# Cluster attention and two MLPs on one core: one transfer for the centroids, and the second pair's preparation moved forward in the opening

## Chip, cores and metric

The kernel runs on one core of a Trainium2 chip. The time is that of the device for one execution, in microseconds (us), and less is better. Engines are called TensorE, VectorE, ScalarE, POOL (GpSimd) and SyncE; in rows they are PE (PEld for its weight loads), DVE, ACT, POOL and SP.

## What is computed

Per batch and head, each query and key is assigned to the nearest of 16 centroids by cosine similarity, and a query attends only to keys of its own cluster. The result goes through two MLPs (softplus, then a hard swish), all in float32.

```python
batch, n_heads, seq, head_dim, n_clusters = 2, 8, 768, 64, 16
q_assign = np.argmax(np.einsum('bhsd,hcd->bhsc', q_n, c_n), axis=-1)   # q_n, k_n, c_n: of length 1
k_assign = np.argmax(np.einsum('bhsd,hcd->bhsc', k_n, c_n), axis=-1)
mask = q_assign[:, :, :, None] == k_assign[:, :, None, :]
scores = np.where(mask, scale * np.matmul(q, k.transpose(0, 1, 3, 2)), -1000000000.0)
attn = softmax(scores)
x = np.matmul(attn, v)                       # then (1536 tokens, 512)
x = softplus(x @ w_in1) @ w_out1             # 512 -> 2048 -> 512
h = x @ w_in2
out = (h * np.clip(h + 3.0, 0.0, 6.0) / 6.0) @ w_out2
```

## The kernel before

**Pairs and steps.** Two heads make a pair, with the 64 dimensions of each on one half of the 128 partitions; there are eight pairs (two batches of four). Float32 values are kept as a high and a low part and a product is the sum of three matmuls (high by high, low by high, high by low). The attention runs in steps: one step `s` is one head's tile of 128 queries, so a pair has 12 steps. In step `s`, in this order: `expo(s+1)` on ScalarE (exponentials of 128 by 768 scores), `row_max(s+2)` on VectorE (tile `nm`), `flip(s, 0)` and `flip(s, 1)` (three transposes each on TensorE into tile `t`, the high part on ScalarE as `pth`, the low part on VectorE as `ptl`), `scores(s+3)` on TensorE (four matmuls), and `weigh` on TensorE (probabilities by v) from step 3 on. The scores have two banks, so scores(s) waits for expo(s-2).

**Order.** The whole attention is in a manual schedule: each engine executes its instructions in the order in which the program writes them. Work beside the steps is put in by `at(s, where, fn)`: it is written at place `where` (0 to 6) of step `s`; place 3 is between the two flips, place 4 behind them and ahead of the scores. The loop begins at step -3, and the first scores(0) are written ahead of it. All transfers but the centroids' are issued by SyncE, in order; SyncE stops at a transfer whose data or target isn't ready, and all later ones stand behind it.

**Preparing a pair.** `load_qk` brings q and k (384 KB each), into one buffer each, so that the next pair's must wait until the low part of this pair's is computed. `p_split_hi` and `p_split_lo` make the parts, a half of 384 columns at a time: high parts of pairs 0 and 1 on ScalarE; low parts of pair 0 and of pair 1's q on VectorE, of pair 1's k on POOL. `p_centroids` writes the pair's centroids into the weights `cwh` and `cwl` (four short POOL steps). `p_sims` is three matmuls of 384 columns; parts 0 and 2 take q's two halves, 1 and 3 k's. `p_sims_out` evacuates them on ScalarE, scaled by the centroids' inverse norms `c_r`, `p_back` transposes them, and five steps on VectorE and POOL (`p_max`, `p_equal`, `p_rank`, `p_best`, `p_first`) give one-hot rows, which `p_onehot` transposes and `p_mask` evacuates. `assemble` copies the parts into the operands Q[i] and K[i] of head i (five transfers between SBUF places, 1.15 MB), and `assemble_mask` adds the one-hot rows (four small ones). Q[0] and K[0] may be overwritten once scores(5) have read them, and scores(12), the first of the second pair, need them again. `p_values` splits v on POOL (four steps for a pair).

**The opening.** The first pair is done differently: its centroids come in five transfers issued by ScalarE (`cT`, transposed, and four copies of the rows `c_sb`), their norms are computed by `c_root` (a logarithm and an exponential on ScalarE, then two rounds of four short VectorE steps) and `c_unit`; Q[0] and K[0] are put together by `assemble_first`, one head is ranked by `one_head(0)` and the other by `one_head(1)` in step 0, and `place` writes the one-hot rows from PSUM straight into Q[0] and K[0]. `warm` are transposes of the identity whose result isn't used. `bank(0, ...)` takes PSUM banks in turn from the list `spare`. The banks of the tag "t" are those that the flips use later.

**Beside it.** Weights of the first MLP are fetched in pieces (`fetch_w`, two transfers of 512 KB) and converted by `convert_abs` (ScalarE), three `convert_bits` (VectorE), `convert_parts` (ScalarE) and `convert_rest` (POOL).

Of the kernel before, what the change touches and what calls it, by code (L numbers as in the profile page):

```python
# [22 lines left out]
def cluster_attention_then_two_mlps(  # L23
# [3 lines left out]
    k: bass.AP,  # L27
    v: bass.AP,
    centroids: bass.AP,
    centroid_rows: bass.AP,  # L30
    w_in1: bass.AP,
    w_out1: bass.AP,
    w_in2: bass.AP,
# [3 lines left out]
    nc = tc.nc  # L37
# [2 lines left out]
    B, NPAIR, _, S = q.shape  # L40
    D = v.shape[-1]
    H = 2 * NPAIR
    C = centroids.shape[-1]
    NJ = S // P
    NT, DM = out.shape
    DFF = w_in1.shape[1]
# [8 lines left out]
    def f32(ap):  # L55
        return ap.bitcast(F32)
# [105 lines left out]
    def attention():  # L162
        with ExitStack() as st, ExitStack() as st_ld, ExitStack() as st_ps:
# [18 lines left out]
            SL = 2 * NJ  # L182
            raws = {}

            def load_qk(n, nm):
                b, p = order[n]
                src = {"q": q, "k": k}[nm]
                t = ld.tile([P, S], F32, tag=nm, name=nm)
                if n == 0:
                    for hf in range(2):  # L190
                        nc.sync.dma_start(t[:, hf * HALF:(hf + 1) * HALF], src[b, p, :, hf * HALF:(hf + 1) * HALF])
                else:
                    nc.sync.dma_start(t, src[b, p])
                raws[n, nm] = t
# [5 lines left out]
                raws[n, "v"] = t  # L200


            cT = cb.tile([P, NPAIR, C], F32, name="cT")
            nc.scalar.dma_start(cT, centroids)
            c_sb = sm.tile([P, HALF], F32, tag="sT", name="c_sb", bufs=1)[:, :NPAIR * D].rearrange("p (n d) -> p n d", d=D)
            for r in range(0, P, 2 * C):
                nc.scalar.dma_start(c_sb[r:r + 2 * C], centroid_rows)
            load_qk(0, "q")
            load_qk(0, "k")

            Q = [qk.tile([P, 2, S], F32R, name=f"Q{i}") for i in range(2)]
# [33 lines left out]
                    pl, tag = ps_p, "prep"  # L245
                return pl.tile(shape, dt, tag=tag, name=name)

            spare = [(ps_t, "t"), (ps_t, "t"), (ps_v, "pv"), (ps_p, "prep")]

            def p_split_hi(n, nm, hf):  # L250
                d = prep.setdefault(n, {})
                if hf == 0:
                    d[nm] = tuple(tp.tile([P, S], F32R, tag=f"{u}{nm}", name=f"{u}{nm}") for u in ("hi", "lo"))
                dst = slice(hf * HALF, (hf + 1) * HALF)
                hi, raw = d[nm][0][:, dst], raws[n, nm][:, dst]
                if n < 2:
                    nc.scalar.activation(hi, raw, AF.Copy, scale=scale if nm == "q" else 1.0)
                else:
                    if nm == "q":
                        nc.gpsimd.tensor_scalar(raw, raw, scale, None, ALU.mult)  # L260
                    nc.gpsimd.tensor_copy(hi, raw)

            def p_split_lo(n, nm, hf):
                d = prep[n]
                dst = slice(hf * HALF, (hf + 1) * HALF)
                hi, lo, raw = d[nm][0][:, dst], d[nm][1][:, dst], raws[n, nm][:, dst]
                if nm == "q" and n < 2:
                    nc.vector.scalar_tensor_tensor(lo, raw, scale, f32(hi), ALU.mult, ALU.subtract)
                else:
                    e = nc.gpsimd if n else nc.vector  # L270
                    e.tensor_tensor(lo, raw, f32(hi), ALU.subtract)
# [239 lines left out]
            def at(s, where, fn, *a):  # L511
                extra.setdefault((s, where), []).append((fn, a))
# [5 lines left out]
            for n in range(NP):  # L518
# [32 lines left out]
                    at(o + 5, 5, p_values, n, 0)  # L551
                    at(o + 6, 4, p_values, n, 1)
                elif n:
                    at(-2, 2, p_split_lo, n, "q", 0)
                    at(-1, 2, p_split_lo, n, "q", 1)
                    at(-1, 1, p_centroids, n)
                    at(-1, 1, p_split_hi, n, "k", 0)
                    at(-1, 1, p_split_lo, n, "k", 0)
                    at(0, 1, p_split_hi, n, "k", 1)
                    at(0, 1, p_split_lo, n, "k", 1)  # L560
                    at(1, 3, p_sims, n, 0)
                    at(1, 3, p_sims, n, 2)
                    at(1, 5, p_sims, n, 1)
                    at(1, 5, p_sims, n, 3)
                    at(2, 1, p_sims_out, n)
                    at(2, 3, p_back, n)
                    at(2, 6, p_max, n)
                    at(3, 2, p_equal, n)
                    at(3, 4, p_rank, n)
                    at(4, 2, p_best, n)  # L570
                    at(5, 2, p_first, n)
                    at(6, 3, p_onehot, n)
                    at(6, 6, p_mask, n)
                    at(5, 3, assemble, n, 0)
                    at(7, 1, assemble_mask, n, 0)
                    at(10, 5, assemble, n, 1)
                    at(11, 4, assemble_mask, n, 1)
                    at(1, 1, load_v, n)
                    at(7, 0, p_values, n, 0)
                    at(10, 3, p_values, n, 1)  # L580
# [56 lines left out]
            for f in range(1, NFA):  # L637
                at(2 * f, 6, fetch_w, 0, f)
            piece = pieces0[0]
            at(2, 0, convert_abs, *piece)  # L640
            at(2, 1, convert_bits, *piece, 0)
            at(2, 3, convert_bits, *piece, 1)
            at(2, 5, convert_bits, *piece, 2)
            at(4, 1, convert_parts, *piece, False)
            at(4, 6, convert_rest, *piece)
            piece = pieces0[1]
            at(7, 0, convert_abs, *piece)
            at(7, 0, convert_bits, *piece, 0)
            at(9, 0, convert_bits, *piece, 1)
            at(11, 4, convert_bits, *piece, 2)  # L650
            at(12, 4, convert_parts, *piece, False)
# [50 lines left out]
                nc.vector.tensor_scalar(c_n, c_n, 1e-6, None, ALU.add)  # L702
                nc.vector.reciprocal(c_r, c_n)

            def assemble_first():

                d = prep[0]
                (qh, ql), (kh, kl) = d["q"], d["k"]
                lo_rows, hi_rows = slice(0, D), slice(D, P)
                nc.gpsimd.tensor_copy(Q[0][lo_rows], qh[lo_rows].unsqueeze(1).to_broadcast([D, 2, S]))  # L710
                nc.sync.dma_start(f32(Q[0])[hi_rows, 0], f32(ql)[lo_rows])
                nc.sync.dma_start(f32(K[0])[hi_rows, 0], f32(kh)[lo_rows])
                nc.scalar.activation(K[0][lo_rows, 0], kh[lo_rows], AF.Copy)
                nc.gpsimd.tensor_copy(K[0][lo_rows, 1], kl[lo_rows])

            p_centroids(0)
            clear(1)
            p_split_hi(0, "q", 0)
            p_split_lo(0, "q", 0)
            p_split_hi(0, "q", 1)  # L720
            p_split_lo(0, "q", 1)
            for step in range(3):
                c_root(step)
            c_unit()
            for hf in range(2):
                p_split_hi(0, "k", hf)
                p_split_lo(0, "k", hf)
            assemble_first()
            load_qk(1, "q")
            load_qk(1, "k")  # L730
            for c in (0, 2, 1, 3):
                p_sims(0, c)
            p_sims_out(0)
            p_back(0)
            load_v(0)
            for _ in range(8):
                nc.tensor.transpose(warm[:, :P], ident, ident)

            oh = sm.tile(full, BF16, tag="oh", name="oh", bufs=1)
            nc.vector.memset(oh, 0.0)  # L740
# [14 lines left out]
                nc.vector.tensor_tensor(ov, eq, mx2.unsqueeze(2).to_broadcast(half), ALU.is_equal)  # L755

            one_head(0)
            po = [None, None]
            for e in range(2):
                p_onehot(0)  # L760
# [17 lines left out]
            place(0, 1, 1)  # L778
            scores(0)
            place(1, 0, 1)  # L780
            assemble(0, 1)
            p_split_hi(1, "q", 0)
            p_split_hi(1, "q", 1)
            p_values(0, 0)
            fetch_w(0, 0)
            p_values(0, 1)
# [197 lines left out]
```

## Time and profile before

| what | value |
|---|---|
| time, median of 3 runs | 794.99 us (794.67 to 795.22) |
| the profiled execution: its time, and its span | 795.4 us, 793.6 us |
| granted TensorE clock, mean | 0.991 of full speed |
| TensorE busy | 772.8 us, 97% |
| VectorE, ScalarE, POOL busy | 462.1, 413.8, 155.0 us |
| moved by DMA | 69.75 MB |

The profile is of one execution. Its span runs from the first to the last instruction; the time of that execution holds the span and 1.8 us around it. Positions are counted from the start of the span. A clock of 1.00 is TensorE's full 2.4 GHz, 0.50 is 1.2 GHz. In the timeline a line may merge several instructions (x3), and what stands in brackets is how long the engine had been idle and what ended that.

### The profile page before, as it was taken

To read this page: it belongs to the slowest core of one execution; us is meant where nothing else is said; L and a number is where in the kernel's file an instruction comes from. 1 tells how busy PE (TensorE), PEld (TensorE's weight loads), DVE (VectorE), ACT (ScalarE), POOL (GpSimd) and SP (SyncE) were. 2 spreads that over 40 slices of the span, in tenths; PEclk is the share of its full clock that TensorE was granted. 3 is DMA by queue.
4 is the path that set the end of the run, shared out by engine and by line. 5 is a ranking of instruction groups with operands and counts; after the bars stand their busy time and mean duration, and the time that the engine had idled before them with its cause. 6 is when DMAs were issued, how large, how long until landed. Compare 5 with 4: busy or idle time off the path is not lost.

```text
span 793.6 us, 10533 instructions
## 1 busy us (share of the span) xinstructions
PE 772.8 (97%) x3829; PEld 645.7 (81%) x3829; DVE 462.1 (58%) x793; ACT 413.8 (52%) x827; POOL 155.0 (20%) x225
## 2 busy tenths in 40 slices
PE   6799999999999999999999999999999999999998
PEld 5688888888888778888888888888888888888886
DVE  4888888888898899921111257779852322232222
ACT  3689889889899766532121344555432222222221
POOL 3467568568423300000000000000000000000000
PEclk8899999999999999999999999999999999999999
DMA  6675484484375390000000265650000100010001
GB/s 156 192 202 136 127 193 110 128 198 109 83 173 190 127 370 1 1 0 1 1 0 1 82 208 178 196 185 1 1 1 0 54 1 0 1 54 0 1 1 53
DMA packets 37876, 69.75 MB, mean 88 GB/s; under 512 B 4384, under 2 KB 22464, under 8 KB 37824
## 3 DMA queue, kind: packets, MB, share of 16 engines
q1 hardware_dynamic: 37488, 68.91, 30.2%
q8 instruction: 30, 0.49, 0.2%
q10 hardware_dynamic: 336, 0.16, 0.1%
q14 instruction: 22, 0.18, 0.1%
HBM read 46.30 MB, written 3.19 MB: 62 GB/s over the span
## 4 chain that ended last, share of the span: by engine, by line
PE 85%; ACT 5%; DVE 4%; DMA 3%; issue 1%; POOL 1%; SPq 0%; ACTq 0%; DVEq 0%; POOLq 0%
PE h L158 32%; PE y L865 17%; PE y L863 16%; PE s L397 6%; PE t L427 6%; PE pv L442 6%; PE psm L297 2%; ACT pr L413 2%; DMA Q<-hiq 1%; ACT pth L431 1%; DMA K<-hik 1%; ACT mk L356 1%; DVE val L108 1%; ACT xs L455 0%; ACT xs L457 0%
## 5 line engine op out<-in xcount | busy, mean ns | idle before, releaser
L158 PE MATMUL h<-xhi,pi 128*128 128x512 f32 x768 | 238.8, 392 | 2.2 <-DVE pi L133 2.2
L158 PEld LDWEIGHTS h<-xhi,pi 128*128 128x128 f32 x768 | 143.7, 188 | 34.3 <-DVE pi L133 3.0
L844 DVE TENSOR_TENSOR glo<-g,ghi 128x512 fp32r<-128x512 f32 x96 | 66.3, 691 | 146.3 <-ACT ghi L831 117.5
L158 PE MATMUL h<-xlo,pi 128*128 128x512 f32 x384 | 150.0, 391 | 0.0
L863 PE MATMUL y<-ghi,po 128*128 128x512 f32 x384 | 118.9, 391 | 0.0
L865 PE MATMUL y<-po,ghi 128*128 128x512 f32 x384 | 118.8, 391 | 0.0
L432 DVE TENSOR_TENSOR ptl<-t,pth 128x384 fp32r<-128x384 f32 x192 | 97.9, 549 | 31.8 <-ACT pth L431 31.6
L837 DVE SCALAR_TENSOR_TENSOR g<-u,h 128x512 f32<-128x512 f32 x48 | 33.0, 687 | 127.2 <-ACT u L833 127.2
L833 ACT ACTIVATE u<-h,half 128x512 f32<-128x512 f32 x48 | 33.0, 686 | 128.3 <-PE h L158 128.1
L397 PE MATMUL s<-K,Q 128*128 128x256 f32 (+1 forms) x384 | 91.8, 361 | 4.5 <-ACT pr L413 3.2
L431 ACT ACTIVATE pth<-t 128x384 fp32r<-128x384 f32 x192 | 85.3, 487 | 17.7 <-PE t L427 17.3
L405 DVE TENSOR_REDUCE nm<-s 128x1 f32<-128x768 f32 x96 | 90.6, 944 | 3.1 <-PE s L397 3.0
L427 PE MATMUL t<-ident,pr 128*128 128x128 f32 x576 | 88.4, 282 | 2.1 <-DVE ptl L432 1.4
L413 ACT ACTIVATE pr<-s,nm 128x768 f32<-128x768 f32 x96 | 86.5, 901 | 3.6 <-DVE nm L405 3.3
L830 ACT ACTIVATE g<-h 128x512 f32<-128x512 f32 x48 | 28.5, 594 | 111.1 <-PE h L158 111.1
L863 PEld LDWEIGHTS y<-ghi,po 128*128 128x128 f32 x384 | 72.0, 188 | 15.7
L158 PEld LDWEIGHTS h<-xlo,pi 128*128 128x128 f32 x384 | 72.1, 188 | 15.6
L865 PEld LDWEIGHTS y<-po,ghi 128*128 128x128 f32 x384 | 72.1, 188 | 15.5
L427 PEld LDWEIGHTS t<-ident,pr 128*128 128x128 f32 x576 | 65.3, 142 | 19.7 <-DVE ptl L432 15.1
L397 PEld LDWEIGHTS s<-K,Q 128*128 128x128 f32 x384 | 67.0, 192 | 15.9 <-ACT pr L413 5.4
L865 PE MATMUL y<-po,glo 128*128 128x512 f32 x192 | 75.1, 391 | 0.0
L863 PE MATMUL y<-glo,po 128*128 128x512 f32 x192 | 75.0, 391 | 0.0
(125 smaller groups left out, 945.8 us busy)
## 6 DMA issues: line engine op xcount, KB each, us to landing
ri<-in_moe_w_in SPq DMA_DIRECT2D x32, 512.0 KB, 4.7
ro<-in_moe_w_out SPq DMA_DIRECT2D x32, 512.0 KB, 5.3
K<-hik SPq DMA_DIRECT2D x31, 192.0 KB, 4.7
Q<-hiq SPq DMA_DIRECT2D x15, 384.0 KB, 4.2
Q<-loq SPq DMA_DIRECT2D x16, 192.0 KB, 5.6
v<-in_v SPq DMA_DIRECT2D x8, 384.0 KB, 3.4
rsb<-row SPq DMA_DIRECT2D x16, 192.0 KB, 4.0
out<-o SPq DMA_DIRECT2D x12, 256.0 KB, 2.0
```

Of the source, the lines that this page charges most:

```text
L158: nc.tensor.matmul(hs[n][:, :TB], w[:, c, :], x[c][:, cols], start=(c == 0 and i == 0), stop=(c == NC - 1 and i == 2))
L397: nc.tensor.matmul(ps[:, n0:n1], Q[i][:, u, j * P:(j + 1) * P], K[i][:, u, n0:n1], start=(u == 0), stop=(u == 1),)
L405: nc.vector.tensor_reduce(nm, st_s[t][:, :S], AX.X, ALU.max, negate=True)
L413: nc.scalar.activation(pr, st_s.pop(t)[:, :S], AF.Exp, bias=st_p[t], accum_out=sums_of[n][:, i, j:j + 1])
L427: nc.tensor.transpose(pt[:, c * P:(c + 1) * P], pr[:, kt * P:(kt + 1) * P], ident)
L431: last_flip[:] = [nc.scalar.activation(dh, src, AF.Copy)]
L432: nc.vector.tensor_tensor(dl, src, f32(dh), ALU.subtract)
L442: nc.tensor.matmul(st_v[h][:, :HALF], vs[:, kt, i, :], st_t[h][u][:, kt, :], start=(kt == 0 and u == 0), stop=(kt == NJ - 1 and u == 1),)
L833: nc.scalar.activation(t["u"], t["h"], AF.Relu, bias=half, scale=1.0 / 6.0)
L844: nc.vector.tensor_tensor(t["glo"], t["g"], f32(t["ghi"]), ALU.subtract)
L863: nc.tensor.matmul(y[:, :TB], w[:, e, :], x, **fl)
L865: nc.tensor.matmul(y, x[:, e * P:(e + 1) * P], w.rearrange("p c e -> p (c e)"), **fl)
```

## The change

- The centroids come in one transfer of 160 KB (transposed ones and four copies of the rows side by side, laid out by the host). SyncE issues it between the two halves of the first q; ScalarE issues none.
- The norms' steps are written between the first pair's splits. The first parts of Q[0] and K[0] are copied by other engines: Q's high part by ScalarE instead of POOL, K's high part by POOL instead of ScalarE; the two transfers of `assemble_first` and the next loads are issued as soon as their half is split. q's similarities are written ahead of k's splits.
- There are 20 warm-up transposes behind the first 15, in two groups, where there were 8.
- The first pair's `pbk` takes the bank of `pv`, and the first `po` the second bank of "t".
- The second pair: the splits of q's parts go ahead of the loop, in between `one_head` and `place`; k's high parts go ahead of the loop, its centroids and low parts to the start of step -3; q's six similarity matmuls to step -1 ahead of scores(2), k's to step 0 between the flips; evacuation and ranking one step earlier; `assemble` of head 0 from step 5 to step 4, its mask from 7 to 6.
- The first weight piece is converted over steps 3 to 7 (2 to 4 before), the second piece begins in step 8 (7 before).

```diff
--- before.py
+++ after.py
@@ -27,7 +27,6 @@
     k: bass.AP,
     v: bass.AP,
     centroids: bass.AP,
-    centroid_rows: bass.AP,
     w_in1: bass.AP,
     w_out1: bass.AP,
     w_in2: bass.AP,
@@ -40,7 +39,7 @@
     B, NPAIR, _, S = q.shape
     D = v.shape[-1]
     H = 2 * NPAIR
-    C = centroids.shape[-1]
+    C = centroids.shape[-1] // NPAIR - D
     NJ = S // P
     NT, DM = out.shape
     DFF = w_in1.shape[1]
@@ -182,13 +181,15 @@
             SL = 2 * NJ
             raws = {}
 
-            def load_qk(n, nm):
+            def load_qk(n, nm, between=None):
                 b, p = order[n]
                 src = {"q": q, "k": k}[nm]
                 t = ld.tile([P, S], F32, tag=nm, name=nm)
                 if n == 0:
                     for hf in range(2):
                         nc.sync.dma_start(t[:, hf * HALF:(hf + 1) * HALF], src[b, p, :, hf * HALF:(hf + 1) * HALF])
+                        if between and hf == 0:
+                            between()
                 else:
                     nc.sync.dma_start(t, src[b, p])
                 raws[n, nm] = t
@@ -200,12 +201,10 @@
                 raws[n, "v"] = t
 
 
-            cT = cb.tile([P, NPAIR, C], F32, name="cT")
-            nc.scalar.dma_start(cT, centroids)
-            c_sb = sm.tile([P, HALF], F32, tag="sT", name="c_sb", bufs=1)[:, :NPAIR * D].rearrange("p (n d) -> p n d", d=D)
-            for r in range(0, P, 2 * C):
-                nc.scalar.dma_start(c_sb[r:r + 2 * C], centroid_rows)
-            load_qk(0, "q")
+            cent = cb.tile([P, NPAIR * (C + D)], F32, name="cent")
+            cT = cent[:, :NPAIR * C].rearrange("p (n c) -> p n c", c=C)
+            c_sb = cent[:, NPAIR * C:].rearrange("p (n d) -> p n d", d=D)
+            load_qk(0, "q", lambda: nc.sync.dma_start(cent, centroids))
             load_qk(0, "k")
 
             Q = [qk.tile([P, 2, S], F32R, name=f"Q{i}") for i in range(2)]
@@ -245,7 +244,7 @@
                     pl, tag = ps_p, "prep"
                 return pl.tile(shape, dt, tag=tag, name=name)
 
-            spare = [(ps_t, "t"), (ps_t, "t"), (ps_v, "pv"), (ps_p, "prep")]
+            spare = [(ps_t, "t"), (ps_v, "pv"), (ps_t, "t"), (ps_p, "prep")]
 
             def p_split_hi(n, nm, hf):
                 d = prep.setdefault(n, {})
@@ -551,28 +550,24 @@
                     at(o + 5, 5, p_values, n, 0)
                     at(o + 6, 4, p_values, n, 1)
                 elif n:
-                    at(-2, 2, p_split_lo, n, "q", 0)
-                    at(-1, 2, p_split_lo, n, "q", 1)
-                    at(-1, 1, p_centroids, n)
-                    at(-1, 1, p_split_hi, n, "k", 0)
-                    at(-1, 1, p_split_lo, n, "k", 0)
-                    at(0, 1, p_split_hi, n, "k", 1)
-                    at(0, 1, p_split_lo, n, "k", 1)
-                    at(1, 3, p_sims, n, 0)
-                    at(1, 3, p_sims, n, 2)
-                    at(1, 5, p_sims, n, 1)
-                    at(1, 5, p_sims, n, 3)
-                    at(2, 1, p_sims_out, n)
-                    at(2, 3, p_back, n)
-                    at(2, 6, p_max, n)
-                    at(3, 2, p_equal, n)
-                    at(3, 4, p_rank, n)
-                    at(4, 2, p_best, n)
-                    at(5, 2, p_first, n)
-                    at(6, 3, p_onehot, n)
-                    at(6, 6, p_mask, n)
-                    at(5, 3, assemble, n, 0)
-                    at(7, 1, assemble_mask, n, 0)
+                    at(-3, 0, p_centroids, n)
+                    at(-3, 0, p_split_lo, n, "k", 0)
+                    at(-3, 0, p_split_lo, n, "k", 1)
+                    at(-1, 3, p_sims, n, 0)
+                    at(-1, 3, p_sims, n, 2)
+                    at(0, 3, p_sims, n, 1)
+                    at(0, 3, p_sims, n, 3)
+                    at(1, 1, p_sims_out, n)
+                    at(1, 3, p_back, n)
+                    at(1, 6, p_max, n)
+                    at(2, 2, p_equal, n)
+                    at(2, 4, p_rank, n)
+                    at(3, 2, p_best, n)
+                    at(4, 2, p_first, n)
+                    at(5, 3, p_onehot, n)
+                    at(5, 6, p_mask, n)
+                    at(4, 3, assemble, n, 0)
+                    at(6, 3, assemble_mask, n, 0)
                     at(10, 5, assemble, n, 1)
                     at(11, 4, assemble_mask, n, 1)
                     at(1, 1, load_v, n)
@@ -637,15 +632,15 @@
             for f in range(1, NFA):
                 at(2 * f, 6, fetch_w, 0, f)
             piece = pieces0[0]
-            at(2, 0, convert_abs, *piece)
-            at(2, 1, convert_bits, *piece, 0)
-            at(2, 3, convert_bits, *piece, 1)
-            at(2, 5, convert_bits, *piece, 2)
-            at(4, 1, convert_parts, *piece, False)
-            at(4, 6, convert_rest, *piece)
+            at(3, 0, convert_abs, *piece)
+            at(3, 1, convert_bits, *piece, 0)
+            at(4, 3, convert_bits, *piece, 1)
+            at(5, 5, convert_bits, *piece, 2)
+            at(6, 1, convert_parts, *piece, False)
+            at(7, 6, convert_rest, *piece)
             piece = pieces0[1]
-            at(7, 0, convert_abs, *piece)
-            at(7, 0, convert_bits, *piece, 0)
+            at(8, 0, convert_abs, *piece)
+            at(8, 0, convert_bits, *piece, 0)
             at(9, 0, convert_bits, *piece, 1)
             at(11, 4, convert_bits, *piece, 2)
             at(12, 4, convert_parts, *piece, False)
@@ -702,39 +697,44 @@
                 nc.vector.tensor_scalar(c_n, c_n, 1e-6, None, ALU.add)
                 nc.vector.reciprocal(c_r, c_n)
 
-            def assemble_first():
-
-                d = prep[0]
-                (qh, ql), (kh, kl) = d["q"], d["k"]
-                lo_rows, hi_rows = slice(0, D), slice(D, P)
-                nc.gpsimd.tensor_copy(Q[0][lo_rows], qh[lo_rows].unsqueeze(1).to_broadcast([D, 2, S]))
-                nc.sync.dma_start(f32(Q[0])[hi_rows, 0], f32(ql)[lo_rows])
-                nc.sync.dma_start(f32(K[0])[hi_rows, 0], f32(kh)[lo_rows])
-                nc.scalar.activation(K[0][lo_rows, 0], kh[lo_rows], AF.Copy)
-                nc.gpsimd.tensor_copy(K[0][lo_rows, 1], kl[lo_rows])
+            lo_rows, hi_rows = slice(0, D), slice(D, P)
+
+            def warm_up(count):
+                for _ in range(count):
+                    nc.tensor.transpose(warm[:, :P], ident, ident)
+
 
             p_centroids(0)
             clear(1)
             p_split_hi(0, "q", 0)
             p_split_lo(0, "q", 0)
             p_split_hi(0, "q", 1)
+            c_root(0)
             p_split_lo(0, "q", 1)
-            for step in range(3):
-                c_root(step)
-            c_unit()
+            nc.sync.dma_start(f32(Q[0])[hi_rows, 0], f32(prep[0]["q"][1])[lo_rows])
+            load_qk(1, "q")
+            c_root(1)
+            for c in (0, 2):
+                p_sims(0, c)
+            warm_up(6)
             for hf in range(2):
                 p_split_hi(0, "k", hf)
                 p_split_lo(0, "k", hf)
-            assemble_first()
-            load_qk(1, "q")
+            nc.sync.dma_start(f32(K[0])[hi_rows, 0], f32(prep[0]["k"][0])[lo_rows])
             load_qk(1, "k")
-            for c in (0, 2, 1, 3):
+            c_root(2)
+            c_unit()
+            for c in (1, 3):
                 p_sims(0, c)
+            nc.scalar.activation(
+                Q[0][lo_rows], f32(prep[0]["q"][0])[lo_rows].unsqueeze(1).to_broadcast([D, 2, S]), AF.Copy
+            )
+            nc.gpsimd.tensor_copy(K[0][lo_rows, 0], prep[0]["k"][0][lo_rows])
+            nc.gpsimd.tensor_copy(K[0][lo_rows, 1], prep[0]["k"][1][lo_rows])
+            load_v(0)
             p_sims_out(0)
             p_back(0)
-            load_v(0)
-            for _ in range(8):
-                nc.tensor.transpose(warm[:, :P], ident, ident)
+            warm_up(14)
 
             oh = sm.tile(full, BF16, tag="oh", name="oh", bufs=1)
             nc.vector.memset(oh, 0.0)
@@ -755,6 +755,9 @@
                 nc.vector.tensor_tensor(ov, eq, mx2.unsqueeze(2).to_broadcast(half), ALU.is_equal)
 
             one_head(0)
+            p_split_hi(1, "q", 0)
+            p_split_hi(1, "q", 1)
+            p_split_lo(1, "q", 0)
             po = [None, None]
             for e in range(2):
                 p_onehot(0)
@@ -778,9 +781,10 @@
             place(0, 1, 1)
             scores(0)
             place(1, 0, 1)
+            p_split_lo(1, "q", 1)
             assemble(0, 1)
-            p_split_hi(1, "q", 0)
-            p_split_hi(1, "q", 1)
+            p_split_hi(1, "k", 0)
+            p_split_hi(1, "k", 1)
             p_values(0, 0)
             fetch_w(0, 0)
             p_values(0, 1)
@@ -964,8 +968,13 @@
         "q": cols(inputs["q"]),
         "k": cols(inputs["k"]),
         "v": inputs["v"].reshape(b, h // 2, 2, p, s // p, d).transpose(0, 1, 3, 4, 2, 5),
-        "centroids": pairs.transpose(1, 3, 0, 2).reshape(2 * d, h // 2, c),
-        "centroid_rows": pairs.transpose(1, 2, 0, 3).reshape(2 * c, h // 2, d),
+        "centroids": np.concatenate(
+            [
+                pairs.transpose(1, 3, 0, 2).reshape(p, -1),
+                np.broadcast_to(pairs.transpose(1, 2, 0, 3), (p // (2 * c), 2, c, h // 2, d)).reshape(p, -1),
+            ],
+            axis=1,
+        ),
     }
     for name in ("moe_w_in", "moe_w_out", "moe2_w_in", "moe2_w_out"):
         laid[name] = inputs[name]
```

## Rows read from the trace of the kernel before

**Rows 1.** The page's first part: busy us, share of the span, instructions.

```profile
PE 772.8 (97%) x3829; PEld 645.7 (81%) x3829; DVE 462.1 (58%) x793; ACT 413.8 (52%) x827; POOL 155.0 (20%) x225
```

**Rows 2.** Windows: each engine's busy us (instructions), TensorE's granted clock, DMA share, GB/s.

```profile
10.00:20.00 10.00, 6.89 (x29) 5.33 (x30) 5.34 (x19) 3.50 (x7) 0.87 (x2) 0.66 0.82 198
...
60.00:70.00 10.00, 10.00 (x66) 8.69 (x65) 8.76 (x16) 9.60 (x23) 7.31 (x12) 1.00 0.36 92
```

**Rows 3.** The chain of waits, opening: start, us, what.

```profile
0.73 2.64 DMA q<-in_q
...
6.57 1.68 DVE c_sq L690
...
8.28 0.43 DVE c_ss L691
...
11.33 0.55 DVE lok L271
...
13.93 0.59 ACT sT L303
...
19.16 0.72 PE s L397 x3
```

**Rows 4.** The chain of waits, 20 to 53 us.

```profile
20.78 1.16 DVE loq L268
...
33.74 0.68 DVE val L108
...
37.20 11.20 DMA Q<-hiq
...
51.84 0.74 PE s L397 x3
```

**Rows 5.** Timeline, two copies: start, us, engine, line, operation, [idle before].

```profile
6.50 1.46 POOL L710 CAST Q<-hiq 64x1536 fp32r<-64x1536 f32 x1
...
10.23 0.84 ACT L713 ACTIVATE K<-hik 64x768 fp32r<-64x768 f32 x1
```

**Rows 6.** Timeline, SyncE and POOL: the way of v.

```profile
12.75 0.42 SPq L199 DMA_DIRECT2D v<-in_v  x1
...
19.95 0.50 POOL L366 CAST vs<-v 128x384 fp32r<-128x384 f32 x1 [6.73 <-DMA v<-in_v]
...
23.33 0.52 POOL L279 CAST cwh<-cT 64x16 fp32r<-64x16 f32 x1
...
24.76 2.08 POOL L271 TENSOR_TENSOR lok<-k,hik 128x384 fp32r<-128x384 f32 x2
```

**Rows 7.** Timeline, TensorE: two similarity matmuls, scores(2), the first of scores(12).

```profile
6.28 0.52 PE L297 MATMUL psm<-hiq,cwh 128*128 128x384 f32 x1
...
6.60 0.52 PE L297 MATMUL psm<-loq,cwh 128*128 128x384 f32 x1
...
21.94 1.65 PE L397 MATMUL s<-K,Q 128*128 128x512 f32 x4 [1.38 <-ACT pr L413]
...
50.84 0.47 PE L397 MATMUL s<-K,Q 128*128 128x512 f32 x1 [0.15 <-DMA K<-hik]
```

**Rows 8.** Windows of one microsecond: fall and return of the granted clock.

```profile
21.00:22.00 1.00, 0.06 (x1) 0.06 (x1) 1.00 (x2) 1.00 (x3) 1.00 (x2) 0.88 1.02 257
22.00:23.00 1.00, 1.00 (x3) 0.81 (x4) 1.00 (x2) 0.46 (x2) 0.92 (x2) 0.50 1.05 219
...
28.00:29.00 1.00, 1.00 (x6) 1.00 (x5) 0.81 (x2) 0.49 (x1) 0.00 (x0) 0.71 0.02 9
```

**Rows 9.** Timeline, VectorE: maxima nm(2), nm(3), nm(5), nm(12).

```profile
25.91 0.94 DVE L405 TENSOR_REDUCE nm<-s 128x1 f32<-128x768 f32 x1
...
27.70 0.94 DVE L405 TENSOR_REDUCE nm<-s 128x1 f32<-128x768 f32 x1
...
35.89 0.94 DVE L405 TENSOR_REDUCE nm<-s 128x1 f32<-128x768 f32 x1
...
52.61 0.96 DVE L405 TENSOR_REDUCE nm<-s 128x1 f32<-128x768 f32 x1
```

## Prediction

> **What bounds the kernel now.** I read four views in this order: the page's busy times, the windows of ten microseconds, the chain of waits over the first 55 us, and the timeline of single engines there. The first says that TensorE is busy for 97% of the span [rows 1], so only a stretch in which it isn't can give anything. The windows show where that is: in 10 to 20 us TensorE is busy for 6.89 of 10, at a granted clock of 0.66, while the DMA engines are at 0.82 and move 198 GB/s; from 60 us it is busy for all 10 [rows 2]. From there on any lead that TensorE has is kept, and nothing later is edited. So the question is how much earlier TensorE reaches the state that it has now at about 52 us, at scores(12), the first scores of the second pair.
>
> The chain says what sets that. Opening: the first half of q lands at 3.37, the norms run on VectorE from 6.57 to 11.33, then the low parts of k, the evacuation of the similarities at 13.93, and full scores from 19.16 [rows 3]. After it: two low parts of the second pair's q on VectorE (the first 1.16), the bit work of a weight piece, and then the transfer of Q's high parts, 11.20 us in a crowded queue, with the mask behind it, for which most of scores(12) wait until 51.84 [rows 4].
>
> **The opening.** The one transfer (160 KB) goes into SyncE's queue behind the first half of q, and ScalarE issues none. First low part done: 3.37, plus 0.5 for the high part (estimate from ScalarE's 0.84 for twice the columns [rows 5]), plus 0.55 [rows 3], is 4.4. The square of the centroids now runs there. It took 1.68, but began with a POOL copy of 1.46 under way and ended 0.28 after that; the reduce over as many elements took 0.43 [rows 3, 5]. POOL has only short work then, so I take 0.43 (ends: 0.43 and 1.68). With 0.43 for the reduce, 0.2 for a small step (2.62 us between 8.71 and 11.33 hold eleven of them on VectorE, two on ScalarE and a cast), the other low part 0.55, four small steps 0.8 and k's two low parts 1.1, VectorE is through at 7.95. POOL's copy of K's high part, moved there from ScalarE, is half of a 1.46 row; if it held both low parts up, 8.7. I take 8.35, against 12.35 before (11.33 plus two times 0.5).
>
> The page "SBUF — State Buffer" of the Trainium skill (section "SBUF: two separate sides") says that VectorE, when it reads two SBUF operands, and POOL share a pair of ports that one instruction holds exclusively to its end. By that rule it would be 8.7, and the forecast below 0.35 later; c_sq's 1.68 agrees with it.
>
> Six small steps later, 9.55, the norms are there and the evacuation starts at 9.7; 5.23 us on as before, full scores at 14.9, 4.2 earlier. Q's copy, moved to ScalarE, costs twice 0.84, hidden: ScalarE is done with k at about 7 and isn't wanted before 9.7. The first two splits of the second pair's q lie in ScalarE's and VectorE's waits for the one-hot transposes. Twenty warm-up transposes instead of eight lie in TensorE's waits; if they came at half speed, fourteen would delay the one-hots by about 1 us, which the next paragraph covers. The other bank order frees the second flip's bank from a VectorE step, worth at most 0.3.
>
> **What the lead meets.** The six similarities of the second pair's q now stand on TensorE before scores(2). They need that pair's centroid weights, which POOL makes after both p_values, and these wait for v. Before, this cost nothing: the similarities stood in step 1. Behind them on TensorE now queue scores(2) and the flips of step 0, for which VectorE's maximum, ScalarE's exponentials and all after them wait. When does v land? It was issued at 12.75, behind the second pair's k, which waits for k's low parts, and POOL started on it at 19.95: 7.2 us [rows 6]. It is now issued at 8.35 + 0.4 = 8.75. But the queue before it holds one transfer more, Q's low part of 192 KB (0.197 MB), which was long through before: 1.0 us at 198 GB/s [rows 2]. So v lands at 16.95. Lower end: 1.57 MB from 6.1 at that rate, and 1.0 for the landing, 15.0; upper end, with c_sq held up, 18.2. POOL's p_values take 3.4 and three of the four centroid steps 1.1 of 1.43 (23.33 and 24.76 [rows 6]): the similarities start at 21.4. TensorE has then been idle for some 5 us.
>
> A matmul of this shape goes by in 0.32 in the slow stretch, 6.28 to 6.60 [rows 7], and the clock does fall after such idleness: it was granted 0.88 and then 0.50 when scores(2) had been waited for, and came back in 28 to 29 us [rows 8], 6.3 us after work resumed at 21.94. So six take 1.95, and scores(2) start at 23.35, **1.4 later than before**, though the first scores came 4.2 earlier.
>
> The page "TensorE: Matmul & The Clock Gate" of the Trainium skill (section "Loop structure matters more than you think") warns of just this: matmuls that stand behind a transfer run at the cold clock. At the full clock these six would take 1.0 instead of 1.95; rows 8 agree with the rule for the stretch of before.
>
> From there, by maxima on VectorE [rows 9]. The third, nm(2): 23.35 + 1.65 = 25.0 against 25.91, as the two low parts and one head's ranking no longer stand in front. Then three flips (0.65), k's six similarities (1.95), the other flips, ScalarE's and VectorE's splits (1.6): nm(3) at 23.35 + 1.4 + 0.65 + 1.95 + 1.6 = 28.95 against 27.70. Up to nm(5) it took 8.19. Two bit steps of 0.68 [rows 4] move behind it, one step of 0.55 moves ahead, and I take about 1.35 less idle time on VectorE, since k's similarities no longer stand between flips and two jobs of ScalarE come later: nm(5) at 35.0 against 35.89. The bits then come back, less the step moved ahead: 52.61 - 35.89 + 0.8 puts nm(12) at 52.5, a lead of 0.1. The opening's lead is nearly gone.
>
> Then scores(12). The five transfers of assemble now go out one step earlier, ahead of a 384 KB and two 512 KB transfers: 1.4 MB, 7 us at 198 GB/s. What is queued behind their wait for scores(5) is the third pair's k, wanted only in step 8. So the wait up to 51.84 goes, and the matmuls follow the one that started at 50.84 [rows 7]: of about 1.0 us I take 0.8 (ends 0 and 1.0, VectorE and ScalarE being almost full there). Last, the clock may return sooner than 6.3 us after 21.4, as the rows hold one return only: 0.4 (ends 0 and 1.5). Sum: -0.1 - 0.8 - 0.4 = -1.3.
>
> The profiled execution took 795.4, its span of 793.6 and 1.8 around it; the median of the runs is 794.99. I put the difference on the median: **793.7**.
>
> **The rivals.**
> *The opening's lead survives.* Scores(2) could start at about 17.6 (14.9, a maximum and an exponential). That needs POOL to be through by then, so v by 13.1. Seven us from issue to landing speak against it. It gives 795.0 - 4.2 = 790.8.
> *The clock is back early.* If it comes 3 us after 21.4 instead of 6.3, k's similarities and the flips behind run at full speed: 1.5 less instead of 0.4, 792.6. For it: the 6.3 is a single observation. Against: it is the only one that the rows have.
> *Slower: v lands no earlier than now.* If the crowded queue holds it until 20, each step above moves by 3.0: 795.0 - 1.3 + 3.0 = 796.7. It decides from 19.9 on. For it: DMA is already at 0.82, and everything is issued earlier into the same engines.
> *No lasting gain.* VectorE and ScalarE hold scores(12) as long as the transfer did: 794.9.
>
> **How the numbers follow.** Likeliest 0.38; survives 0.14; early clock 0.27; slower 0.09; no lasting gain 0.12. About 0.2%, 1.6 us, is what a measurement can tell. Faster than 793.4: 0.14 + 0.27 and 0.05 of the likeliest, 0.46. Slower than 796.6: 0.09. Same: 0.45. The likeliest's own range, from v at 15.0 or 18.2, is 792.2 to 795.2; 8 in 10 is 790.6 to 795.9, without the slower case and the outer half of the surviving one.
>
> **What would show it.** First full scores near 14.9; v's wait on POOL ending near 17; TensorE idle from about 16 to 21, ended by POOL's centroids, and the clock at 0.50 after; scores(2) near 23.3; no wait for K's mask at scores(12). It is wrong if v lands before 14, or if scores(12) still wait.

## The result: 0.65% slower, and the profile after

The changed kernel took 799.40 us (median of four runs) against 794.83 for the kernel before (median of four): ratio 1.0065, 95% interval 1.0053 to 1.0077, where the two medians alone give 1.0057. The forecast was 793.7, within 790.6 to 795.9. The profiled execution took 800.72, its span 798.9; before, it was 795.4 and 793.6. Three of the kernels below had one execution far from their others (951 us in a_valother, 1542 in a_openonly, 4338 in b_conv), and all times here are medians of the others.

The timeline of the changed kernel, with single instructions of SyncE, POOL, TensorE, VectorE and ScalarE (start, us, engine, line, operation; in brackets the idle time before it and what ended it):

```profile
15.32 1.40 PE L396 MATMUL s<-K,Q 128*128 128x512 f32 x7 [0.72 <-ACT K L777]
...
17.59 0.50 POOL L365 CAST vs<-v 128x384 fp32r<-128x384 f32 x1 [7.93 <-DMA v<-in_v]
...
21.74 0.69 PE L296 MATMUL psm<-hiq,cwh 128*128 128x384 f32 x1 [5.02 <-POOL cwh L278]
...
23.82 1.49 PE L396 MATMUL s<-K,Q 128*128 128x512 f32 x4
...
25.34 0.96 DVE L404 TENSOR_REDUCE nm<-s 128x1 f32<-128x768 f32 x1 [5.18 <-PE s L396]
...
28.85 0.95 DVE L404 TENSOR_REDUCE nm<-s 128x1 f32<-128x768 f32 x1
...
34.82 0.94 DVE L404 TENSOR_REDUCE nm<-s 128x1 f32<-128x768 f32 x1
...
35.47 0.38 SPq L194 DMA_DIRECT2D q<-in_q  x1
...
43.35 1.17 POOL L259 TENSOR_SCALAR q<-q 128x384 f32<-128x384 f32 x1 [7.57 <-DMA Q<-loq]
...
45.91 0.95 PE L396 MATMUL s<-K,Q 128*128 128x512 f32 x4
...
50.47 1.26 POOL L132 TENSOR_TENSOR pi<-val,pi 128x512 fp32r<-128x512 f32 x1
...
51.77 0.67 ACT L97 ACTIVATE val<-ro 128x512 f32<-128x512 f32 x1 [5.08 <-POOL pi L132]
...
53.36 1.65 PE L396 MATMUL s<-K,Q 128*128 128x512 f32 x4 [5.16 <-ACT pr L412]
...
58.66 0.95 DVE L404 TENSOR_REDUCE nm<-s 128x1 f32<-128x768 f32 x1
```

Up to 46 us this is the forecast. Full scores start at 15.32 instead of 19.16 [rows 3]. POOL's wait for v ends at 17.59 (16.95 in the forecast), TensorE's wait for the centroids at 21.74 (21.4), scores(2) start at 23.82 (23.35), nm(2) at 25.34 (25.0), nm(3) at 28.85 (28.95) and nm(5) at 34.82 (35.0), against 25.91, 27.70 and 35.89 before [rows 9]. Scores(10) start at 45.91. Then it breaks: scores(11) don't start until 53.36, after 5.16 us in which TensorE is idle, and nm(12) comes at 58.66 instead of 52.61. TensorE waited for an exponential of ScalarE, ScalarE had been idle for 5.08 us at `convert_abs` of the second weight piece (`val<-ro`), and that waited for POOL's `convert_rest` of the first (`pi<-val,pi`).

The chain of waits of the changed kernel over the same stretch (start, us, what) says what stood before that on POOL:

```profile
9.19 8.28 DMA v<-in_v
...
21.74 2.29 PE psm L296 x6
24.03 1.28 PE s L396 x4
...
36.65 6.71 DMA Q<-loq
43.37 1.16 POOL q L259
...
47.73 1.15 POOL q L259
...
50.47 1.27 POOL pi L132
51.77 0.67 ACT val L97
52.43 0.89 ACT pr L412 x2
53.36 1.65 PE s L396 x4
```

The third pair's q is scaled and split on POOL from 43.37 and again from 47.73, with a half of v between them, and only then comes the weight piece's last step. (The rows name `Q<-loq` for what POOL waited for before 43.37; q's own load, issued at 35.47, landed 7.7 us later, at about 43.2, and it is q that POOL reads there.) There is one buffer `val` for the converted values (`val0` has one), and this last step is its last reader; the next piece's first step writes it. Before, that last step stood at (4, 6) and the next first step at (7, 0). The change puts them at (7, 6) and (8, 0).

Windows of the changed kernel (TensorE's busy time, weight loads, VectorE, ScalarE, POOL, granted clock, DMA share, GB/s) show the clock around the two waits:

```profile
20.00:21.00 1.00, 0.00 (x0) 0.00 (x0) 0.16 (x1) 0.00 (x0) 1.00 (x2) 0.54 1.11 273
...
26.00:27.00 1.00, 1.00 (x5) 1.00 (x5) 0.80 (x2) 0.47 (x1) 0.00 (x0) 0.55 0.00 0
27.00:28.00 1.00, 1.00 (x8) 0.92 (x7) 0.06 (x1) 0.15 (x1) 0.00 (x0) 1.00 0.00 0
...
51.00:52.00 1.00, 0.00 (x0) 0.00 (x0) 0.00 (x0) 0.23 (x1) 1.00 (x2) 0.50 0.00 0
...
57.00:58.00 1.00, 1.00 (x6) 0.92 (x5) 0.28 (x1) 1.00 (x4) 0.00 (x0) 0.69 0.49 56
```

Both times it falls to 0.50 while TensorE waits (0.54 is the mean of the microsecond in which it fell), and TensorE works at half speed for some 5 and some 4 us afterwards.

### The profile page after: what moved, and what is told of

It reads as the page before. It is cut to its first block, busy times and chain, and to the rows that moved or that the text cites. A ratio compares the mean times of both kernels' runs of the same rounds, so it can differ in the third digit from the quotient of the medians.

```text
span 798.9 us, 10545 instructions
## 1 busy us (share of the span) xinstructions
PE 773.1 (97%) x3841; PEld 646.6 (81%) x3841; DVE 461.7 (58%) x793; ACT 414.0 (52%) x827; POOL 154.7 (19%) x225
## 4 chain that ended last, share of the span: by engine, by line
PE 85%; ACT 5%; DMA 3%; DVE 2%; POOL 2%; issue 1%; SPq 0%; ACTq 0%; DVEq 0%; POOLq 0%
PE h L157 32%; PE y L869 16%; PE y L867 16%; PE s L396 6%; PE t L426 6%; PE pv L441 6%; PE psm L296 2%; ACT pr L412 2%; ACT pth L430 1%; DMA v<-in_v 1%; DMA Q<-loq 1%; DMA K<-hik 1%; ACT mk L355 1%; ACT xs L454 0%; DMA q<-in_q 0%
```

## The experiments

Three theories for the loss. **A:** the shared buffer `val`, as just described. **B:** POOL's lateness as such, which follows from the late landing of the third pair's q; with or without `val`, it would hold the next similarities. **C:** the late scores(2) of the opening. Others came up on the way: **D**, that transfers or VectorE hold the steps up to scores(12) whatever is done before, and for the wait at scores(12) **E** and **F** below. A label with `a_` or `best_` is the changed kernel with an edit, `b_conv` is the kernel before with one, and `after_again` is the changed kernel itself, run once more. Kernels of one group ran on one chip, so each is compared with the kernel before on that chip. The ratios come from the runs and not from the two medians, so they can differ from the medians' by 0.1%.

| kernel | us | before | ratio, 95% interval |
|---|---|---|---|
| a_restdve | 794.39 | 793.72 | 1.0011, 1.0002 to 1.0020 |
| a_convold | 794.89 | 793.72 | 1.0018, 1.0009 to 1.0028 |
| b_conv | 795.63 | 793.72 | 1.0034, 1.0020 to 1.0048 |
| a_pool | 793.35 | 793.72 | 1.0000, 0.9990 to 1.0009 |
| after_again | 799.67 | 793.88 | 1.0071, 1.0052 to 1.0090 |
| a_valother | 793.97 | 793.88 | 1.0001, 0.9989 to 1.0014 |
| a_pool_valother | 788.19 | 793.88 | 0.9929, 0.9907 to 0.9950 |
| a_openonly | 790.88 | 793.88 | 0.9964, 0.9954 to 0.9974 |
| a_val_fetch | 793.81 | 794.08 | 0.9997, 0.9988 to 1.0007 |
| a_val_fetch_busy | 792.91 | 794.08 | 0.9994, 0.9978 to 1.0010 |
| best_fetch | 788.36 | 794.08 | 0.9927, 0.9911 to 0.9944 |
| openonly_look | 789.99 | 794.08 | one run |

### Is it the buffer?

**a_restdve**, the last step on another engine:

```diff
-            at(7, 6, convert_rest, *piece)
+            at(7, 6, lambda *a: convert_rest(*a, engine=nc.vector), *piece)
```

> The changed kernel, with one step of the weight piece, convert_rest at (7, 6), on VectorE instead of POOL; nothing else. Theory A (the one buffer val is freed only by convert_rest, which in the changed kernel stands on POOL behind the third pair's splits, so that ScalarE waits 5.1 us for it in step 8 and all after): the wait goes, and with it the stretch at the half clock behind it; 792.5 to 794.5, no idle stretch of ScalarE at 47 to 52 us. Rival B (POOL's lateness itself, through the third pair's q landing late, would hold the next pair's similarities whatever val does): 797 or more. Rival C (the late scores(2) of the opening are the loss): no change, 799.

794.39: 0.11% above before instead of 0.65 to 0.71%. Between 4 and 5 us come back, as A says; B and C predicted 797 and more. I had expected no wait to be left; it falls from 5.08 to 1.34 us, in the timeline of a_restdve:

```profile
47.12 0.67 ACT L97 ACTIVATE val<-ro 128x512 f32<-128x512 f32 x1 [1.34 <-DVE pi L132]
```

**a_valother**, the buffer taken out of it and nothing moved (POOL stays as late as it was):

```diff
-        val = wpools["val"].tile([P, NC, P], F32, tag="val", name="val")
+        if (layer, f, nm) == (0, 0, "o"):
+            val = wpools["sm"].tile([P, S], F32, tag="rsb", name="val2", bufs=1)[:, :NC * P].rearrange(
+                "p (c e) -> p c e", c=NC)
+        else:
+            val = wpools["val"].tile([P, NC, P], F32, tag="val", name="val")
...
+            wpools["sm"] = sm
```

> The changed kernel, with the second weight piece's converted values in another buffer (that of rsb, which is free until step 16); convert_rest stays late on POOL. Theory A (the shared buffer val is what is waited for): the wait in step 8 goes and the time is that of the run with convert_rest on VectorE, 0 to 0.2% above the kernel before. Rival B (POOL's lateness as such): 0.4% or more above it.

> The changed kernel itself, beside the next three on one chip: 0.5 to 0.8% above the kernel before, with ScalarE's wait of about 5 us in step 8. All theories say the same here; it is the base for the others.

793.97 beside 799.67 for the changed kernel on the same chip (in the trace of after_again ScalarE waited 4.02 us in step 8, where the first one had 5.08). In the timeline of a_valother the second piece's first step no longer waits; it runs 3.46 us ahead of POOL's last step of the first:

```profile
43.99 0.66 ACT L100 ACTIVATE val<-ro 128x512 f32<-128x512 f32 x1
...
47.45 1.71 POOL L135 TENSOR_TENSOR pi<-val,pi 128x512 fp32r<-128x512 f32 x1
47.67 0.47 PE L400 MATMUL s<-K,Q 128*128 128x512 f32 x1
...
50.22 0.71 PE L400 MATMUL s<-K,Q 128*128 128x512 f32 x3 [2.08 <-DMA K<-mk]
...
52.83 1.63 PE L400 MATMUL s<-K,Q 128*128 128x512 f32 x4
...
56.83 0.85 PE L400 MATMUL s<-K,Q 128*128 128x512 f32 x4
```

So A holds and B falls: the shared buffer costs 5.7 us (799.67 - 793.97). The rows from 47.67 on are for later: scores(12) still wait for a mask, and scores(13) and scores(14) follow.

**a_convold** gives the weight pieces their old places in the changed kernel, **b_conv** gives the kernel before the new places alone (the edit of a_convold is shown; that of b_conv is its reverse, in the kernel before):

```diff
-            at(3, 0, convert_abs, *piece)
-            at(3, 1, convert_bits, *piece, 0)
-            at(4, 3, convert_bits, *piece, 1)
-            at(5, 5, convert_bits, *piece, 2)
-            at(6, 1, convert_parts, *piece, False)
-            at(7, 6, convert_rest, *piece)
+            at(2, 0, convert_abs, *piece)
+            at(2, 1, convert_bits, *piece, 0)
+            at(2, 3, convert_bits, *piece, 1)
+            at(2, 5, convert_bits, *piece, 2)
+            at(4, 1, convert_parts, *piece, False)
+            at(4, 6, convert_rest, *piece)
             piece = pieces0[1]
-            at(8, 0, convert_abs, *piece)
-            at(8, 0, convert_bits, *piece, 0)
+            at(7, 0, convert_abs, *piece)
+            at(7, 0, convert_bits, *piece, 0)
```

> The changed kernel, with the first two weight pieces converted in the places of before (steps 2 to 4, and from 7). Theory A: convert_rest runs on POOL while POOL waits for the third pair's q, so no wait in step 8; 793 to 795.5, as the bit steps are back in the crowded step 2. Rival B: 797 or more. Rival C: 799.

> The kernel before, with only the new places of the weight pieces. Theory A: convert_rest comes behind the third pair's q and v on POOL, which is through with them at about 47.8, and the second piece's convert_abs would come at about 47: a wait of some 2 us, 796 to 798. Rival B (late landing caused by the earlier assemble): no change, 795. Rival C: no change, 795.

794.89 and 795.63. The old places remove most of the loss too (0.18% of it is left), and the new places alone cost the kernel before 0.34%. There the wait is shorter than I expected, 0.90 us instead of 2, in the timeline of b_conv:

```profile
42.10 0.63 ACT L122 ACTIVATE pi<-val 128x512 fp32r<-128x512 f32 x1 [1.45 <-DVE val L112]
...
46.25 1.28 POOL L133 TENSOR_TENSOR pi<-val,pi 128x512 fp32r<-128x512 f32 x1
...
47.56 0.68 ACT L98 ACTIVATE val<-ro 128x512 f32<-128x512 f32 x1 [0.90 <-POOL pi L133]
```

The wait for the buffer is thus only part of b_conv's loss. Its trace shows one more that comes with the new places: in step 6 `convert_parts` waits 1.45 us for the last bit step on VectorE, and TensorE is idle for 1.55 us behind it; what that costs was not tried. That the buffer's wait is 0.90 here and 5.08 in the changed kernel goes with when the third pair's q is there: POOL starts on it at 38.69 in b_conv and at 43.35 in the changed kernel, where it is issued 2.4 us later and the second pair's `assemble` right behind it (its landing took 7.7 us, against 5.4 in b_conv).

### Where the opening's lead went

**a_pool** lets the second pair's centroids and low parts go ahead of `p_values` on POOL, so that TensorE's similarities don't hang on v. **a_pool_valother** has that and the other buffer. **a_openonly** keeps only the changed opening and has the second pair's schedule, its splits and the weight pieces of before; **openonly_look** is one more execution of it, whose trace is used.

```diff
-            p_values(0, 0)
             fetch_w(0, 0)
-            p_values(0, 1)
+            at(-3, 1, p_values, 0, 0)
+            at(-3, 1, p_values, 0, 1)
```

> The changed kernel, with the second pair's centroids and low parts of k ahead of the first pair's p_values on POOL. Theory A: TensorE no longer waits for v before scores(2), which start near 17.6 instead of 23.8, but the wait in step 8 stays, as it hangs on the third pair's q and POOL: 795 to 798. Rival C (the opening's stall is the whole loss): 793 or less.

> The changed kernel with both: the other buffer for the second piece, and the second pair's centroids and low parts ahead of p_values on POOL. If the two waits are all that eats the opening's lead of 4 us: 0.5 to 1.0% below the kernel before (787 to 790). If transfers or VectorE hold the steps up to scores(12) as well (rival D): within 0.3% of it.

> The changed opening alone (one centroid transfer, norms between the parts, copies on other engines, banks, warm-ups), with the second pair's schedule and the weight pieces of before. The similarities stand in step 1 again, so TensorE doesn't wait for v before scores(2). If the opening's lead of 4 us is real and only what was moved forward ate it: 0.2 to 0.5% below the kernel before. If it is lost later anyhow (rival D): within 0.15%.

> A second look at the run with the changed opening alone, for its trace: first full scores near 15, scores(2) near 17.5 without a wait for POOL, the second pair's similarities in step 1, and a lead over the kernel before that shrinks from 4 us to about 3 by scores(12).

a_pool took 793.35: level with before although the wait for the buffer is still in it. I had expected 795 to 798 by A and 793 or less by C, so here A's figure missed and C's was close. Timeline of a_pool:

```profile
18.45 0.96 PE L396 MATMUL s<-K,Q 128*128 128x512 f32 x4 [0.44 <-ACT pr L412]
...
42.93 1.26 POOL L132 TENSOR_TENSOR pi<-val,pi 128x512 fp32r<-128x512 f32 x1
...
44.22 0.66 ACT L97 ACTIVATE val<-ro 128x512 f32<-128x512 f32 x1 [4.22 <-POOL pi L132]
```

Scores(2) start at 18.45 instead of 23.82 and run in 0.96 instead of 1.49 us, at a granted clock of 1.00 from 14 to 24 us. With both waits gone, 788.19: 0.71% below the kernel before. So the wait for v costs 5.8 us (793.97 - 788.19), as much as the buffer, and the two add up: with both the ratio is 1.0071, without the one or the other 1.0001 and 1.0000, without both 0.9929. Either wait alone makes the difference between a loss and a level time, so A and C both hold as costs. What sets them apart is that the forecast had counted the wait for v, and not the buffer. D falls. Timeline of a_pool_valother:

```profile
16.75 0.34 PE L300 MATMUL psm<-hiq,cwh 128*128 128x384 f32 x1
...
43.70 0.47 PE L400 MATMUL s<-K,Q 128*128 128x512 f32 x1
44.68 0.71 PE L400 MATMUL s<-K,Q 128*128 128x512 f32 x3 [0.51 <-DMA K<-mk]
```

The opening alone is worth 3.0 us (790.88 against 793.88), and there scores(2) run at 18.22, in the trace of openonly_look:

```profile
15.44 1.40 PE L396 MATMUL s<-K,Q 128*128 128x512 f32 x7 [0.72 <-ACT K L778]
18.22 1.65 PE L396 MATMUL s<-K,Q 128*128 128x512 f32 x4 [1.38 <-ACT pr L412]
```

The lead of 4 us is real, and most of it stays as long as nothing stands before scores(2) that needs v. What was moved forward then gains nearly as much again once both waits are gone (0.9929 in a_pool_valother against 0.9964).

### The wait at scores(12), and the clock

I had counted 0.8 us for scores(12) no longer waiting for the mask, and a_valother showed them waiting for 2.08. **a_val_fetch** moves the third fetch of weights behind the mask, in a_valother; **best_fetch** does so in a_pool_valother. **a_val_fetch_busy** adds unused transposes to a_val_fetch, to keep TensorE at work while it waits for POOL.

```diff
-                at(2 * f, 6, fetch_w, 0, f)
+                at((2, 6)[f - 1], 6, fetch_w, 0, f)
```

In a_val_fetch_busy alone:

```diff
+            def keep_busy():
+                t = ps_p.tile([P, 512], F32, tag="prep", name="busy")
+                for _ in range(36):
+                    nc.tensor.transpose(t[:, :P], ident, ident)
+
+            at(-1, 2, keep_busy)
```

> The changed kernel with the other buffer for the second weight piece, and the third fetch of weights (two transfers of 512 KB) at (6, 6) instead of (4, 6), so that the mask's four transfers at (6, 3) no longer queue behind it. Theory E (scores(12) still wait for the mask, 2.5 us in the run without this move, since only the big transfers went ahead of the 1.4 MB and the mask did not): the wait goes, 0.15 to 0.35% below the kernel before. Rival F (ScalarE and VectorE hold the steps there anyhow): within 0.1% of the kernel before.

> All three: the other buffer, the second pair's centroids ahead of p_values on POOL, and the third fetch behind the mask. Theory E: another 0.1 to 0.2% below the 0.9929 of the run without the fetch's move, as its scores(12) waited 1.0 us for the mask: 0.991 to 0.992. Rival F: 0.993.

> The same, with 36 transposes of the identity, whose result isn't used, on TensorE ahead of the second pair's similarities, where it waits for POOL. If half speed after that wait is worth what the rows say (six matmuls at 0.32 and scores(2) at 1.5 instead of 0.7): the clock stays at 1.00, the maximum of step 1 comes 1.5 to 2.5 us sooner, and the time is 0.1 to 0.25% below the run without them. If the wait for POOL alone counts: equal to it.

The mask's wait at scores(12) goes in a_val_fetch and in best_fetch, but the times don't show it: 0.9997 against 1.0001, and 0.9927 against 0.9929. E's mechanism is right and its price is wrong. The waits were also shorter than the 2.5 and 1.0 us that I set down for them: 2.08 in a_valother and 0.51 in a_pool_valother. What is gained there meets the next wait of its kind, at scores(18), for the mask of the pair's second head. Timeline of best_fetch:

```profile
44.03 0.94 PE L400 MATMUL s<-K,Q 128*128 128x512 f32 x4
...
61.17 0.70 PE L400 MATMUL s<-K,Q 128*128 128x512 f32 x3 [1.09 <-DMA K<-mk]
```

In a_val_fetch the same wait is 0.85, in a_pool_valother 0.49; before and in a_valother there is none. In the traces, a_val_fetch leads the kernel before by 1.6 us at scores(17) (62.70 against 64.34) and by 0.8 at scores(19) (68.33 against 69.13). That the wait absorbs the gain is argued from these rows; a kernel without it was not tried.

The transposes do keep the clock up. Windows of a_val_fetch, without them:

```profile
18.00:20.00 2.00, 0.00 (x0) 0.00 (x0) 1.62 (x5) 0.81 (x2) 1.92 (x3) 0.78 1.05 226
20.00:22.00 2.00, 0.66 (x2) 0.66 (x3) 0.00 (x0) 0.00 (x0) 1.72 (x6) 0.50 1.08 322
```

and of a_val_fetch_busy, with them:

```profile
18.00:20.00 2.00, 2.00 (x21) 2.00 (x20) 1.90 (x4) 1.03 (x4) 1.84 (x5) 1.00 1.06 259
20.00:22.00 2.00, 1.85 (x13) 1.64 (x12) 0.56 (x2) 0.00 (x0) 1.80 (x5) 1.00 1.07 359
```

The third maximum, nm(2), comes at 22.82 instead of 24.94; 0.7 us of that is v's earlier landing in this execution (POOL starts on it at 16.44, against 17.18). The whole kernel is 0.9 us faster by the medians, but its ten runs spread from 790.8 to 797.0, and the intervals of the two ratios (0.9988 to 1.0007, and 0.9978 to 1.0010) cover each other: what the clock alone is worth stays open, and the runs can't tell a gain of up to some 2 us from none. The fastest version is a_pool_valother, with best_fetch equal to it: 0.7% below the kernel before.

## Why the prediction was wrong

**The step that failed** is "The bits then come back, less the step moved ahead: 52.61 - 35.89 + 0.8 puts nm(12) at 52.5". It priced the weight piece's move by its steps on VectorE and ScalarE. The piece's last step, `convert_rest`, moved too, on POOL's queue from ahead of the third pair's splits to behind two of them, and to one place ahead of the step that needs its buffer. I named what is queued behind SyncE's and TensorE's moved steps, and never asked what stands ahead of this one on POOL, nor which buffer it frees. In the sum the term stood at nothing. The runs put it at 5.7 us (a_valother against the changed kernel); nm(12) came at 58.66.

**The wait for v: right, and it decided the sum.** Its working held to 0.7 us at each step up to nm(5). Some 0.4 of the lateness arose early: k's two low parts were through on VectorE at 8.79, close to the 8.7 given for the case that POOL's copy holds them up, and not at the 8.35 taken (rows in the last section). The lower end of 15.0 for v had 1.0 us for its landing that no row gives; the earliest start of POOL on v in these traces is 16.00, in a_valother. The rival that the opening's lead survives fell for the reason given, v's landing; a_pool_valother, without that wait and without the buffer's, took 788.19 and so kept the lead.

**The wait at scores(12): wrong.** "So the wait up to 51.84 goes" left out that the mask's own four transfers stay behind the 1.4 MB that the big ones were moved ahead of. In a_valother, which is the changed kernel without the failed step, the wait is 2.08, longer than before. There scores(12) go on 1.6 us ahead of before (50.22 against 51.84), but the clock falls to 0.50 behind the wait, scores(13) take 1.63 us, and scores(14) at 56.83 have no lead left (56.87 before). That kernel is level with before (0.9989 to 1.0014), where my sum had 1.3 us less (0.9984). Yet a_val_fetch, without the wait, is no nearer to my sum beyond the noise (0.9997), so which of the sum's small terms made up that difference stays open. In the changed kernel itself scores(12) don't wait, as they come some 5 us late.

**The clock: right in kind.** It fell in the wait as forecast. It came back 5 us after work resumed at 21.74 in the changed kernel, between the 6.3 of before and the 3 of the rival.

**The rival on the other side was the wrong one.** I had a slower case at 0.09, by v landing late. v landed when expected, and the kernel was slower by a wait that none of my rivals had.

## What to carry to other kernels

When a step is moved in a kernel whose order is written by hand, follow every instruction of it on every engine, the slow helper engine too: what stands ahead of it there now, and which buffer it is the last to read. A buffer with one copy makes a dependency that no data shows, and its slack is the number of steps between its last reader and its next writer; here it went from two to none.

A lead is worth what the first shared wait leaves of it. Four microseconds won in the opening were all given back at one in-order queue (POOL, behind v), and came back when the lines that wait for v were moved behind those that TensorE needs.

## What the hardware showed that was not expected

A short VectorE step can be held up by POOL as much as a long one: multiplying two tiles of 128x4 took 0.16 us at 6.64 in the changed kernel, and 0.78 at 8.90, with a POOL copy of 0.82 running from 8.84. The two low parts of k before it, 1.01 together in the kernel before, took 1.67 beside a POOL copy of 1.21:

```profile
6.64 0.16 DVE L692 TENSOR_TENSOR c_r<-c_r,c_ss 128x4 f32<-128x4 f32 x1
...
7.12 1.67 DVE L270 TENSOR_TENSOR lok<-k,hik 128x384 fp32r<-128x384 f32 x2
7.15 1.21 POOL L732 CAST K<-hik 64x768 fp32r<-64x768 f32 x1 [0.47 <-ACT hik L256]
...
8.84 0.82 POOL L733 CAST K<-lok 64x768 fp32r<-64x768 f32 x1 [0.48 <-DVE lok L270]
8.90 0.78 DVE L692 TENSOR_TENSOR c_r<-c_r,c_ss 128x4 f32<-128x4 f32 x1
```

The short step ended as the copy did, which agrees with the exclusive pair of ports of the Trainium skill's page "SBUF — State Buffer" (section "SBUF: two separate sides").

A transfer seems to land later for what is issued behind it: the third pair's q, 384 KB, took 5.8 us before and 7.7 in the changed kernel, with 1.15 MB of copies between SBUF places right behind it in the same queue. The other traces lean the same way, but meet: 5.4 to 6.6 us in the three that keep the old order (b_conv, openonly_look, a_openonly), and 6.5 to 7.6 in the nine that have the copies right behind. No run moved the copies alone, so this stays a reading and isn't shown.
